# A one-token attention and MLP mix: the output row kept as four columns per partition and stored from there

## The chip, the cores and the metric

The kernel runs on one core of one Trainium2 chip. The metric is the device time of one execution in microseconds (us). The core has a matrix engine (TensorE, PE in the profile), VectorE (DVE), ScalarE (ACT), GpSimd (POOL) and SyncE (SP), each with its own stream of instructions; they meet only through semaphores. SP, ACT and POOL also issue DMAs, which sixteen DMA engines carry out. Matrix products take their weights and their moving data from the on-chip memory SBUF (128 partitions) and leave results in PSUM (128 partitions, eight banks).

## The reference, cut to what matters

One token `x` (512 numbers) goes through two branches, which a sigmoid gate `g` mixes. Branch A is attention with 32 heads of width 128 against a cache of 4096 keys and values per head; branch B is a two-layer MLP with a squared ReLU.

```python
g = sigmoid((x * gate_w).sum(-1, keepdims=True))
q = (x @ wq).reshape(32 heads, 128)
p = softmax(q @ k_cache^T * 128 ** -0.5)          # 32 x 4096
a = concat_heads(p @ v_cache) @ wo                # 4096 -> 512
h = relu(x @ w1 + b1) ** 2                        # 512 -> 1376
b = h @ w2 + b2                                   # 1376 -> 512
out = g * a + (1 - g) * b                         # 512 numbers, bf16
```

The two caches are 32 MiB each in bf16, `wq` and `wo` 4 MiB each, so the work is mostly the reading of some 78 MB.

## The kernel before, in words

The heads are taken in eight tiles of four (`NT = 8`). A ring of five slots of 4 MiB (`ring`, `SLOTS`) receives the K and V tiles in the order of `LOADS`; SP issues them, each when the slot's former owner has been used up (`free`). For a K tile DVE forms part of the scores itself (line 711) and PE turns the rest with a matmul against the identity (line 509) and multiplies it with the query columns (line 522); ACT forms the exponentials (line 434); PE multiplies with V (`pv`, line 553). The order on every engine is written out by hand in the blocks at the end of each engine's function.

The last stage is the one that the change touches. The output has 512 numbers, and the sums of all output products stand in one small PSUM tile, `acc`, 128 partitions by 4 columns: output number `n` is at partition `n % 128`, column `n // 128`. Five groups of products add to it, every one a 128 by 128 block of weights with one moving column, four blocks (`j = 0..3`) for the four columns:

- `out_a` (line 580): heads 0 to 27 with `wo`, for 22 of the 32 rows that a partition of `W` holds; the other ten rows are summed on DVE (`rows_v`, line 777) into `vsum` and added to `acc` by `add_v` (line 586), four fp32 matmuls with a column of ones.
- `mlp_out(n)` (line 605): the eleven blocks of `w2`; the first ten run before the last V products, the eleventh (`w2b`) at the very end.
- `out_b` (line 614): heads 28 to 31 with `wob_sb`, sixteen matmuls, after the last V products, their normalisation on DVE (`norm`, line 741) and the arrival of `wob_sb`.

The last three loads on SP's queue are the two parts of `wob_sb` (line 339) and `w2b` (line 341). PE's order at the end is: ten `mlp_out`, `pv(28)`, `add_v`, `pv(29)`, `pv(30)`, `pv(31)`, then `out_b`, then `mlp_out(10)`. Behind them the result is finished in four steps: DVE adds the gated bias `b2g` and rounds to bf16 (`fin`, line 814); PE turns the 128 by 4 tile into 4 rows of 128 (line 667); DVE copies these rows from PSUM to SBUF (`fin4`, line 816); SP stores the four rows, 256 bytes each (line 343), and waits for the store (line 819).

At the start, ACT issues four small loads, the last of which is `b2` as 4 rows of 128 (line 394); PE turns it into four columns with one small matmul (line 465), ahead of the eleven that turn `b1` (line 467) and of the query products (line 487).

Of the kernel before, what the change touches and what calls it, by code (L numbers as in the profile page):

```python
# [5 lines left out]
def bass_gated_mix__gqa_block_cached__dense_activation_squared_relu__decode_kernel(  # L6
# [15 lines left out]
    fp32 = mybir.dt.float32  # L22
# [7 lines left out]
    DM = 512  # L30
# [104 lines left out]
    with ctx:  # L135
# [21 lines left out]
        W4 = W3 + DM  # L157
        W5 = W4 + NZ * DM
        wob_sb = held("m")[:, W4:W5].rearrange("p (h n) -> p h n", h=NZ)
        oA, fin4 = [held("m")[0:p, W5 + n * 128:W5 + n * 128 + 128] for n, p in enumerate((NA, 4))]  # L160
        vsum = held("k", NT - 1)[:, 0:2 * DM].bitcast(fp32)


# [4 lines left out]
            at[0] += n  # L168
            return start[0:p, at[0] - n:at[0]]

        xrow, grow, b1r, b2r = early(1, DM), early(1, DM), early(1, F), early(4, 128)
        zeros = early(128, 128)
        xb = early(128, 4 * 128).rearrange("p (t n) -> p t n", t=4)

# [32 lines left out]
        b2g = sb("b2g", [128, 4], fp32)  # L207
        fin = sb("fin", [128, 4], bf16)

        KP = [pb(f"KP{i}", [128, HM * 128], bf16) for i in range(3)]  # L210
        pS = pb("pS", [128, 512], fp32)
        pM = pb("pM", [128, 512], fp32)
# [8 lines left out]
        Q = pM[:, 192:192 + NH]  # L221
        Z = pX[:, 0:1]
        XC = pO[:, 0:4]
        B2 = KP[2][:, 0:4]
        QR = [pQ, pX]
        H = pX[:, 256:256 + FG + 1]
        B1 = pM[:, 288:288 + FG + 1]
# [21 lines left out]
        s_at = sem("s_at")  # L249
        s_ac = sem("s_ac")  # L250
        s_b2 = sem("s_b2")
        s_fT = sem("s_fT")
        s_f4 = sem("s_f4")
        s_id = sem("s_id")
        s_cst = sem("s_cst")
        s_xc = sem("s_xc")
# [60 lines left out]
        @block.sync  # L317
        def _(eng):
            for n, (kind, j) in enumerate(LOADS):
                free(eng, n)  # L320
                if n == SLOTS - 1:
                    started(eng)
                    for p, st, k, q in STRIPS[len(RUNS):]:
                        a, b = W[p:p + st * (k - 1) + 1:st, :], woa_v[q:q + k, :]
                        if k == 1:
                            a, b = [v.rearrange("p (a n) -> p a n", a=2) for v in (a, b)]
                        eng.dma_start(a, b).then_inc(s_wr, 16)
                if kind == "v" and j in PARTS:
                    for w in range(len(PARTS[j]) - 1):
                        part = slice(PARTS[j][w] * 128, PARTS[j][w + 1] * 128)  # L330
                        eng.dma_start(held("v", j)[:, part], v_v[j][:, part]).then_inc(s_vl[j, w], 16)  # L331
                elif kind in "kv":
                    eng.dma_start(held(kind, j), (k_v if kind == "k" else v_v)[j])\
                       .then_inc(s_l[n % SLOTS], 16)
                elif kind == "m":
                    eng.dma_start(held("m")[:, 0:W2], w1_v).then_inc(s_w[0], 16)
                    eng.dma_start(held("m")[:, W2:W3], w2_v).then_inc(s_w[1], 16)  # L337
            for c in range(len(TS) - 1):
                eng.dma_start(wob_sb[:, TS[c]:TS[c + 1], :], wob_v[:, TS[c]:TS[c + 1], :])\
                   .then_inc(s_wo[c], 16)  # L340
            eng.dma_start(w2b, B_w2[F - 128:F, :]).then_inc(s_w[2], 16)
            eng.wait_ge(s_f4, 1)
            eng.dma_start(out[0, 0, :].rearrange("(j p) -> j p", p=128), fin4).then_inc(s_out, 16)


        @block.gpsimd
# [42 lines left out]
        @block.scalar  # L389
        def _(eng):  # L390
            eng.dma_start(xrow, A_x[0, :, :]).then_inc(s_x, 16)
            eng.dma_start(grow, gate_w.rearrange("(a n) -> a n", a=1)).then_inc(s_x, 16)
            eng.dma_start(b1r, B_b1.rearrange("(a n) -> a n", a=1)).then_inc(s_b, 16)
            eng.dma_start(b2r, B_b2.rearrange("(j p) -> j p", p=128)).then_inc(s_b, 16)
            eng.wait_ge(s_xc, 1)
            eng.activation(xcolf[:, :], XC, ACT.Copy).then_inc(s_xf, 1)
            eng.wait_ge(s_xf, 1)
            eng.activation(xcol[:, :], xcolf[:, :], ACT.Copy).then_inc(s_xf, 1)
            eng.wait_ge(s_z, 1)
            eng.activation(ez[:, :], Z, ACT.Exp, scale=-1.0).then_inc(s_ez, 1)  # L400

            def qb_copy(c):
                eng.wait_ge(s_qps, c + 1)
                for r in range(R):
                    rows = slice(P * r, P * r + P)
                    eng.activation(qb[rows, c, :], QR[c % 2][rows, r * 128:r * 128 + 128], ACT.Copy)\
                       .then_inc(s_qb, 1)

            def evac(u):
                for j in range(2):  # L410
                    n = 2 * u + j
                    if n >= NC:
                        eng.wait_ge(s_sh, n - NC + 1)
                    eng.wait_ge(s_t, n + 1)
                    eng.activation(kT[:, n % NC, 0:HB[u // U] * 128],  # L415
                                   KP[n % 3][:, 0:HB[u // U] * 128], ACT.Copy).then_inc(s_ev, 1)

            def sc_copy(j):
                eng.wait_ge(s_sh, 2 * U * (j + 1))
                for r in range(R):  # L420
                    rows = slice(P * r, P * r + P)
                    eng.activation(S[rows, j % NS, XT[j]:B], S2[j % 2][rows, r:U * YB[j] * R:R], ACT.Copy).then_inc(s_cp, 1)

            def exps(j):
                eng.wait_ge(s_mb, j + 1)
                eng.activation(nM[:, j:j + 1], MB[:, j:j + 1], ACT.Copy).then_inc(s_nm, 1)  # L426
                eng.wait_ge(s_nm, j + 1)
                if j == 0:
                    eng.wait_ge(s_cst, 3)
                if j >= NE:  # L430
                    eng.wait_ge(s_pv, U * (j - NE + 1))
                for r in range(R):
                    rows = slice(P * r, P * r + P)
                    eng.activation(E[rows, j % NE, :, r], S[rows, j % NS, :], ACT.Exp,  # L434
                                   bias=nM[rows, j:j + 1], scale=SCALE,
                                   accum_out=RS[rows, R * j + r:R * j + r + 1]).then_inc(s_e, 1)

            for c in range(EARLY):
                qb_copy(c)
            for i in range(NU + 2):  # L440
                if i >= U and i % U == 0:
                    sc_copy(i // U - 1)
                if i < NU:
                    evac(i)
                if i == NU - U:
                    exps(NT - 2)
                if EARLY + i < NT:
                    qb_copy(EARLY + i)
                if i > U and i % U == 1 and i != NU - U + 1:
                    exps(i // U - 1)  # L450
# [3 lines left out]
        def _(eng):  # L454
# [7 lines left out]
            eng.matmul(Z, onesf[0:1, :], zp[:, :], start=True, stop=True).then_inc(s_z, 1)  # L462
            eng.wait_ge(s_id, 4)
            eng.wait_ge(s_b, 32)
            eng.transpose(B2, b2r, ident[0:4, 0:4]).then_inc(s_b2, 1)
            for n in range(FG + 1):
                mm = eng.matmul(B1[:, n:n + 1], b1r[:, n:FG * 128:FG] if n < FG else b1r[:, F - 128:F],
                                ident[0:1, 0:1], start=True, stop=True)
# [114 lines left out]
            def add_v():  # L583
                eng.wait_ge(s_vs, TV)
                for j in range(4):
                    eng.matmul(acc[:, j:j + 1], vsum[:, j * 128:(j + 1) * 128], onesf[:, 0:1],
                               start=False, stop=False, skip_group_check=True)

            def mlp_h():
                eng.wait_ge(s_w[0], 16)  # L590
# [7 lines left out]
            def mlp_out(n):  # L598
                if n in (0, FG):
                    eng.wait_ge(s_w[1 if n < FG else 2], 16)  # L600
                if n == 0:
                    eng.wait_ge(s_hs, 1)
                w = w2a[:, n, :] if n < FG else w2b
                for j in range(4):
                    mm = eng.matmul(acc[:, j:j + 1], w[:, j * 128:(j + 1) * 128], hs[:, n:n + 1],
                                    start=False, stop=(n == FG), skip_group_check=True)
                if n == FG:
                    mm.then_inc(s_acc, 1)
# [1 line left out]
            def out_b(c):  # L610
                eng.wait_ge(s_wo[c], 16)
                for h in range(TS[c], TS[c + 1]):
                    for j in range(4):
                        eng.matmul(acc[:, j:j + 1], wob_sb[:, h, j * 128:(j + 1) * 128],  # L614
                                   onorm[:, NA + h:NA + h + 1], start=False, stop=False,
                                   skip_group_check=True)

# [40 lines left out]
            for u in range((NT - 1) * U, NU):  # L658
                if u == NU - 3:
                    add_v()  # L660
                pv(u)
            eng.wait_ge(s_on, NG)
            for c in range(len(TS) - 1):
                out_b(c)
            mlp_out(FG)
            eng.wait_ge(s_fin, 1)
            eng.transpose(KP[2][0:4, 0:128], fin[:, :], ident[:, :]).then_inc(s_fT, 1)


        @block.vector  # L670
        def _(eng):
# [20 lines left out]

            eng.wait_ge(s_b1, 1)
            eng.tensor_copy(b1c[:, :], B1).then_inc(s_b1c, 1)
            eng.wait_ge(s_dz, 3)
            eng.tensor_scalar(omw[:, :], omw[:, :], omg[:, 0:1], None, ALU.mult).then_inc(s_g, 1)

# [110 lines left out]
            gmax(NT - 1)  # L808
            rows_v()
            recip(NG - 1)  # L810
            norm(NG - 1)
            eng.wait_ge(s_acc, 1)
            eng.wait_ge(s_g, 4)
            eng.tensor_tensor(fin[:, :], acc[:, 0:4], b2g[:, :], ALU.add).then_inc(s_fin, 1)
            eng.wait_ge(s_fT, 1)
            eng.tensor_copy(fin4, KP[2][0:4, 0:128]).then_inc(s_f4, 1)

        inner.close()
        nc.sync.wait_ge(s_out, 16)
# [28 lines left out]
```

## Time and profile before

| what | us |
|---|---|
| median of 3 runs (193.01 to 193.13) | 193.02 |
| the profiled execution, its own time | 192.9 |
| span of the profiled execution | 191.5 |
| DVE busy in the span | 159.0 (83%) |
| PE busy in the span | 111.0 (58%) |
| data read from memory | 78.35 MB, 409 GB/s over the span |
| granted TensorE clock after the start | 0.5 of full speed |

The span is the stretch from the first to the last recorded instruction; the execution's own time lies 1.4 us above it. Section 2 of the page cuts the span into 40 slices of 4.8 us and gives each engine's busy share in tenths. The chain is the work that ended last, followed back from the end: every piece of it was released by the one before it. A line of the timeline gives the start, the duration, the engine, the source line, the operation, its tiles and, in brackets, how long the engine had been idle and what released it. PEld is the loading of weights into the matrix engine, SPq the queue on which SP issues DMAs.

### The profile page before, as it was taken

What the parts mean: (1) busy time and instruction counts of PE and PEld (TensorE: products, weight loads), DVE (VectorE), ACT (ScalarE), POOL (GpSimd) and SP (SyncE); (2) the same over time, 40 slices, a digit from 0 to 9 for tenths busy, and PEclk for the clock granted to TensorE, in tenths of its full rate; (3) what the DMA queues carried; (4) which work ended last, traced back from release to release, by engine and by line L of the source; (5) the groups of instructions that cost most, each with busy time, mean ns of one, the idle gap of its engine ahead of it and who ended that gap; (6) DMA issues with size and microseconds to landing.
All of it is one profiled execution on the core that took longest, in us unless ns stands there. A gap on an engine that the chain in (4) does not pass through costs nothing.

```text
span 191.5 us, 6005 instructions
## 1 busy us (share of the span) xinstructions
PE 111.0 (58%) x2058; PEld 97.6 (51%) x2058; DVE 159.0 (83%) x1387; ACT 82.7 (43%) x204; POOL 22.7 (12%) x56
## 2 busy tenths in 40 slices
PE   0129667545614653397569145933887478648975
PEld 0123335535503542297459145933877268537964
DVE  0320399999999999899999998998999799998821
ACT  2105765843833663087349222941663393000400
POOL 7760000996000000000000000000000000000000
PEclk9999985855555555555555555555555555555555
DMA  6999999999999999999999999999999999999992
GB/s 226 432 438 438 438 440 428 438 411 450 411 443 411 421 412 421 438 429 431 414 447 421 428 426 428 431 417 424 428 419 424 411 428 409 421 415 428 417 382 70
DMA packets 5488, 78.74 MB, mean 411 GB/s; under 512 B 1285, under 2 KB 1927, under 8 KB 2056
## 3 DMA queue, kind: packets, MB, share of 16 engines
q1 hardware_dynamic: 4484, 75.40, 92.9%
q0 software_dynamic: 960, 2.95, 3.9%
q8 instruction: 16, 0.26, 0.6%
q14 instruction: 14, 0.11, 0.1%
q10 hardware_dynamic: 14, 0.01, 0.0%
HBM read 78.35 MB, written 0.00 MB: 409 GB/s over the span
## 4 chain that ended last, share of the span: by engine, by line
DVE 48%; DMA 40%; SPq 7%; PE 3%; issue 1%; DVEq 0%
DVE ring L711 45%; DMA ring<-in_A_k_cache_dram 26%; DMA ring<-in_A_wo_dram 14%; SPq L331 6%; DVE S L711 2%; PE pO L553 1%; PE KP L509 1%; DVE gm L725 1%; DVE gx L728 0%; PE pM L562 0%; PE pM L534 0%; PE pQ L614 0%; SPq L337 0%; SPq L294 0%; DVE mp L718 0%
## 5 line engine op out<-in xcount | busy, mean ns | idle before, releaser
L711 DVE CUSTOM_DVE_ANT_0 ring<-ring,qb 128x128 bf16<-128x128 bf16 x656 | 140.6, 280 | 2.9 <-DMA ring<-in_A_k_cache_dram 2.9
L415 ACT ACTIVATE kT<-KP 128x768 bf16<-128x768 bf16 (+1 forms) x64 | 46.4, 783 | 48.1 <-PE KP L509 47.8
L509 PE MATMUL KP<-ident,ring 128*128 128x128 bf16 x368 | 43.4, 302 | 23.2 <-DMA ring<-in_A_k_cache_dram 19.9
L711 DVE DVE_READ_ACCUMULATOR2_ANT S<- 128x1 f32 x656 | 49.7, 76 | 0.1
L509 PEld LDWEIGHTS KP<-ident,ring 128*128 128x128 bf16 x368 | 36.0, 140 | 25.9 <-DMA ring<-in_A_k_cache_dram 20.4
L553 PE MATMUL pO<-E,ring 128*128 128x4 bf16 x640 | 19.5, 167 | 2.9 <-DMA ring<-in_A_v_cache_dram 1.9
L553 PEld LDWEIGHTS pO<-E,ring 128*128 128x128 bf16 x640 | 18.7, 105 | 3.4 <-DMA ring<-in_A_v_cache_dram 2.1
L434 ACT ACTIVATE E<-S,nM 32x128 bf16<-32x128 f32 x32 | 18.5, 580 | 0.9
L553 PE MATMUL pX<-E,ring 128*128 128x4 bf16 x384 | 12.0, 167 | 4.6 <-DMA ring<-in_A_v_cache_dram 4.6
L553 PEld LDWEIGHTS pX<-E,ring 128*128 128x128 bf16 x384 | 11.4, 105 | 5.1 <-DMA ring<-in_A_v_cache_dram 4.9
L426 ACT ACTIVATE nM<-pM 128x1 f32<-128x1 f32 x8 | 1.4, 172 | 23.0 <-PE pM L534 23.0
L529 PE MATMUL pM<-identf,mp 128*1 128x128 f32 x8 | 3.1, 384 | 13.0 <-DVE mp L718 13.0
L534 PE MATMUL pM<-onesf,gx 1*128 1x1 f32 x16 | 4.6, 357 | 8.9 <-DVE gx L728 8.9
L534 PEld LDWEIGHTS pM<-onesf,gx 1*128 1x128 f32 x16 | 4.0, 306 | 9.6 <-DVE gx L728 9.6
L522 PE MATMUL pQ<-qcol,kT 128*128 128x4 bf16 x176 | 7.8, 170 | 1.0 <-ACT kT L415 0.9
L522 PEld LDWEIGHTS pQ<-qcol,kT 128*128 128x128 bf16 x176 | 7.6, 111 | 1.4 <-ACT kT L415 1.4
L434 ACT ACTIVATION_READ_ACCUMULATOR E<-S,nM 32x1 f32 x32 | 8.1, 253 | 0.0
L522 PE MATMUL pS<-qcol,kT 128*128 128x4 bf16 x192 | 8.1, 169 | 0.0
L386 POOL MEMSET tick<- 1x1 f32 x1 | 0.1, 88 | 66.8 <-DMA W<-in_A_wo_dram 66.8
L378 POOL DMA_DIRECT2D W<-in_A_wo_dram x14 | 8.0, 572 | 0.0
L529 PEld LDWEIGHTS pM<-identf,mp 128*1 128x1 f32 x8 | 0.7, 92 | 14.2 <-DVE mp L718 14.0
L522 PEld LDWEIGHTS pS<-qcol,kT 128*128 128x128 bf16 x192 | 7.8, 108 | 0.2
(83 smaller groups left out, 97.3 us busy)
## 6 DMA issues: line engine op xcount, KB each, us to landing
ring<-in_A_k_cache_dram SPq DMA_DIRECT2D x8, 4096.0 KB, 30.4
ring<-in_A_v_cache_dram SPq DMA_DIRECT2D x5, 4096.0 KB, 29.7
W<-in_A_wq_dram SPq DMA_DIRECT2D x1, 4096.0 KB, 12.4
ring<-in_A_v_cache_dram SPq DMA_DIRECT2D x2, 2048.0 KB, 27.7
ring<-in_A_v_cache_dram SPq DMA_DIRECT2D x4, 1024.0 KB, 27.5
ring<-in_A_v_cache_dram SPq DMA_DIRECT2D x2, 1280.0 KB, 31.4
W<-in_A_wo_dram POOLq DMA_DIRECT2D x2, 768.0 KB, 17.8
ring<-in_B_w_dram SPq DMA_DIRECT2D x1, 1376.0 KB, 24.8
```

Of the source, the lines that this page charges most:

```text
L331: eng.dma_start(held("v", j)[:, part], v_v[j][:, part]).then_inc(s_vl[j, w], 16)
L378: eng.dma_start(W[p:p + st * (k - 1) + 1:st, :], woa_v[q:q + k, :], max_dma_last_dim=16384).then_inc(s_wp[n], 16)
L415: eng.activation(kT[:, n % NC, 0:HB[u // U] * 128], KP[n % 3][:, 0:HB[u // U] * 128], ACT.Copy).then_inc(s_ev, 1)
L426: eng.activation(nM[:, j:j + 1], MB[:, j:j + 1], ACT.Copy).then_inc(s_nm, 1)
L434: eng.activation(E[rows, j % NE, :, r], S[rows, j % NS, :], ACT.Exp, bias=nM[rows, j:j + 1], scale=SCALE, accum_out=RS[rows, R * j + r:R * ...
L509: mm = eng.transpose(KP[n % 3][:, y * 128:(y + 1) * 128], held("k", j)[:, b * 128:(b + 1) * 128], ident[:, :])
L522: mm = eng.matmul(S2[j % 2][:, c:c + R], kT[:, n % NC, y * 128:(y + 1) * 128], qcol[:, R * j:R * j + R], start=True, stop=True)
L529: eng.transpose(MT[0:1, :], mp[:, j:j + 1], identf[:, :]).then_inc(s_mt, 1)
L534: eng.matmul(MB[:, j:j + 1], gx[0:1, j % 2, :], onesf[0:1, 0:1], start=True, stop=True).then_inc(s_mb, 1)
L553: mm = eng.matmul(O(R * j, R * j + R), held("v", j)[:, b * 128:(b + 1) * 128], E[:, j % NE, b, :], start=(b == 0), stop=(b == B - 1), skip ...
L711: ins = eng.tensor_tensor_reduce(kb, kb, qb[:, j, :], 1.0, 0.0, ALU.mult, ALU.add, S[:, j % NS, b:b + 1])
L725: eng.tensor_reduce(g, MT[0:1, :].rearrange("a (r p) -> a r p", r=R), AX.X, ALU.max)\
```

## The change

The output is kept in another layout: output number `n` is at partition `n // 4`, column `n % 4`, so that partition `p` holds four neighbouring numbers, and the store takes them straight from `fin`, 128 partitions of 8 bytes.

- The products of the last stage, `out_b` and `mlp_out(10)`, take every fourth column of the weights (`j:DM:4`) and add to a new PSUM tile `last`, in this layout.
- All other products still go to `acc`, in the old layout. `add_v` now closes it and signals. DVE then forms `wide` (128 by 4 by 32, fp32): `acc` spread along a mask `four`, where `four[p, i]` is 1 for `p // 4 == i`. PE multiplies `wide` as weights with a second mask `rest` (`rest[p, j]` is 1 for `p % 4 == j`), which starts `last` with these sums in the new layout (`turn`). `wide` stands on DVE between the last `recip` and the last `norm`; `turn` on PE between `pv(29)` and `pv(30)`.
- The two masks are made on DVE at the start, by two reductions of the fp32 identity, behind the copy of `b1c`.
- `b2` is loaded as one row and turned into the new layout by four one-row matmuls, into `pS` in place of `KP[2]`.
- The turning matmul on PE, the copy to `fin4` on DVE and their two semaphores are gone.

```diff
-        oA, fin4 = [held("m")[0:p, W5 + n * 128:W5 + n * 128 + 128] for n, p in enumerate((NA, 4))]
+        oA = held("m")[0:NA, W5:W5 + 128]
+        wide = held("m")[:, W5 + 128:W5 + 384].bitcast(fp32).rearrange("p (j i) -> p j i", j=4)
...
-        xrow, grow, b1r, b2r = early(1, DM), early(1, DM), early(1, F), early(4, 128)
+        xrow, grow, b1r, b2r = early(1, DM), early(1, DM), early(1, F), early(1, DM)
...
+        four = sb("four", [128, 32], fp32)
+        rest = sb("rest", [128, 4], fp32)
...
-        B2 = KP[2][:, 0:4]
+        B2 = pS[:, 0:4]
+        last = pS[:, 64:68]
...
-            eng.wait_ge(s_f4, 1)
-            eng.dma_start(out[0, 0, :].rearrange("(j p) -> j p", p=128), fin4).then_inc(s_out, 16)
+            eng.wait_ge(s_fin, 1)
+            eng.dma_start(out[0, 0, :].rearrange("(p j) -> p j", p=128), fin[:, :]).then_inc(s_out, 16)
...
-            eng.dma_start(b2r, B_b2.rearrange("(j p) -> j p", p=128)).then_inc(s_b, 16)
+            eng.dma_start(b2r, B_b2.rearrange("(a n) -> a n", a=1)).then_inc(s_b, 16)
...
-            eng.transpose(B2, b2r, ident[0:4, 0:4]).then_inc(s_b2, 1)
+            for t in range(4):
+                mm = eng.matmul(B2[:, t:t + 1], b2r[:, t:DM:4], ident[0:1, 0:1], start=True, stop=True)
+            mm.then_inc(s_b2, 1)
...
             def add_v():
                 eng.wait_ge(s_vs, TV)
                 for j in range(4):
-                    eng.matmul(acc[:, j:j + 1], vsum[:, j * 128:(j + 1) * 128], onesf[:, 0:1],
-                               start=False, stop=False, skip_group_check=True)
+                    mm = eng.matmul(acc[:, j:j + 1], vsum[:, j * 128:(j + 1) * 128], onesf[:, 0:1],
+                                    start=False, stop=True, skip_group_check=True)
+                mm.then_inc(s_cv, 1)
+
+            def turn():
+                eng.wait_ge(s_wd, 1)
+                eng.matmul(last, wide[:, :, :].rearrange("p j i -> p (j i)"), rest[:, :],
+                           start=True, stop=False, skip_group_check=True)
...
-                w = w2a[:, n, :] if n < FG else w2b
                 for j in range(4):
-                    mm = eng.matmul(acc[:, j:j + 1], w[:, j * 128:(j + 1) * 128], hs[:, n:n + 1],
+                    w = w2a[:, n, j * 128:(j + 1) * 128] if n < FG else w2b[:, j:DM:4]
+                    mm = eng.matmul((acc if n < FG else last)[:, j:j + 1], w, hs[:, n:n + 1],
                                     start=False, stop=(n == FG), skip_group_check=True)
...
-                        eng.matmul(acc[:, j:j + 1], wob_sb[:, h, j * 128:(j + 1) * 128],
+                        eng.matmul(last[:, j:j + 1], wob_sb[:, h, j:DM:4],
...
+                if u == NU - 2:
+                    turn()
                 pv(u)
...
-            eng.wait_ge(s_fin, 1)
-            eng.transpose(KP[2][0:4, 0:128], fin[:, :], ident[:, :]).then_inc(s_fT, 1)
...
+            eng.wait_ge(s_id, 4)
+            eng.tensor_reduce(four[:, :], identf[:, :].rearrange("p (i j) -> p i j", j=4), AX.X, ALU.max)\
+               .then_inc(s_fr, 1)
+            eng.tensor_reduce(rest[:, :], identf[:, :].rearrange("p (i j) -> p j i", j=4), AX.X, ALU.max)\
+               .then_inc(s_fr, 1)
...
             recip(NG - 1)
+            eng.wait_ge(s_cv, 1)
+            eng.wait_ge(s_fr, 2)
+            eng.tensor_tensor(wide[:, :, :], acc[:, 0:4].unsqueeze(2).to_broadcast([128, 4, 32]),
+                              four[:, :].unsqueeze(1).to_broadcast([128, 4, 32]), ALU.mult).then_inc(s_wd, 1)
             norm(NG - 1)
             eng.wait_ge(s_acc, 1)
             eng.wait_ge(s_g, 4)
-            eng.tensor_tensor(fin[:, :], acc[:, 0:4], b2g[:, :], ALU.add).then_inc(s_fin, 1)
-            eng.wait_ge(s_fT, 1)
-            eng.tensor_copy(fin4, KP[2][0:4, 0:128]).then_inc(s_f4, 1)
+            eng.tensor_tensor(fin[:, :], last, b2g[:, :], ALU.add).then_inc(s_fin, 1)
```

## The prediction

> **What bounds the kernel now.** I read the page's slices first, then the chain in order of time near its end, then the timeline of the last microseconds, and last the DMA view of the store.
>
> The slices say that the whole span but its last slice is DMA-bound: the DMA row stands at 9 nearly everywhere, and the granted TensorE clock (PEclk) is 0.9 and more in the first five slices (to 24 us) and 0.5 from the ninth on.
>
> ```profile
> PEclk9999985855555555555555555555555555555555
> DMA  6999999999999999999999999999999999999992
> ```
>
> The chain says what is left when the loads run out. Columns are start, duration, what. A load of the last weights lands at 188.56; from there to the store it is 16 products, 4 products, the add, the turning matmul and the copy.
>
> ```profile
> 162.59 25.97 DMA ring<-in_A_wo_dram
> 188.56 0.14 issue
> 188.70 0.57 PE pQ L614 x16
> 189.26 0.28 PE pQ L605 x4
> 189.54 0.02 issue
> 189.57 0.17 DVE fin L814
> 189.74 0.04 issue
> 189.78 0.28 PE KP L667
> 190.07 0.02 issue
> 190.09 0.21 DVE ring L816
> ```
>
> The timeline has the store's issue, the list of waits has SP's last one (0.4 us, for the store), and the DMA view from 190.3 to 191.5, in 40 slices of 0.03 us, the store's eight packets (four of data, four that signal): they run from 191.08 to 191.17, and the span ends at 191.5.
>
> ```profile
> 190.33 0.29 SPq L343 DMA_DIRECT2D out_dram<-ring  x1
> ...
> SPq L819 <- DMA out_dram<-ring: 0.4, 1, 0.4
> ...
> GB/s 0 0 0 0 0 0 0 0 0 0 0 0 0 0 0 0 0 0 0 0 0 0 0 0 0 0 17 9 9 0 0 0 0 0 0 0 0 0 0 0
> ...
> q1 hardware_dynamic: 8, 0.00, 0.5%
> ```
>
> So the store takes 191.5 - 190.33 = 1.17 us from issue to end, and everything that the change does to the end is in 188.56 to 191.5. One wait is not in the chain: `w2b` is issued at 172.27 and its row for line 341 says 16.9 us to landing, which is 189.2. The four `mlp_out` products start at 189.26 because of that load, not because of the sixteen before them.
>
> **Part 1, removed: the turning matmul and the copy.** The store now waits for `fin` (end 189.74) in place of the copy (190.09 + 0.21 = 190.30). Nothing lies beside these steps. The gap from release to issue, 0.03, stays. Term: 189.74 - 190.30 = **-0.56 us**, and SP issues at 189.77.
>
> **Part 2, the strided weights.** The trace has weights with a step of ten elements (lines 594 and 467) and of four (line 459), and contiguous ones (line 614):
>
> ```profile
> 8.11 0.26 PE L459 MATMUL pO<-ident,ring 1*128 1x1 bf16 x4 [8.11 <-DMA ring<-in_gate_w_dram]
> 13.12 0.74 PE L467 MATMUL pM<-ident,ring 1*128 1x1 bf16 x11
> 176.83 2.60 PE L594 MATMUL pX<-xcol,ring 128*128 128x1 bf16 x44
> 188.70 0.57 PE L614 MATMUL pQ<-onorm,ring 128*128 128x1 bf16 x16 [0.55 <-DMA ring<-in_A_wo_dram]
> ```
>
> The pace is (stretch - one duration) / (count - 1), with durations 0.167, 0.192, 0.197 and 0.165 of the source views: step four 31 ns, step ten 55 and 56 ns, contiguous 27 ns. Step ten has one pace at a granted clock of 1.0 (13 us, one row of weights) and of 0.5 (177 us, 128 rows), so neither clock nor rows enter, and the row with the same step, 31 ns, is the nearest. The sixteen products then need 188.67 + 16 x 0.031 = 189.17, still before `w2b` at 189.2: nothing. The four behind it: 4 x 0.004 = **+0.02**. The upper end is 56 ns: the sixteen end at 188.67 + 16 x 0.056 = 189.57, 0.31 after 189.26, and the four cost 4 x 0.029 = 0.12, together +0.43. The lower end is 0.
>
> The Trainium skill, SBUF — State Buffer, section "Door 1: The DMA port swizzle", says that accesses run at full bandwidth with at least two hits in a 16-byte line. A step of four bf16 is 8 bytes, two hits; a step of ten is 20 bytes, one. By that rule the term is 0 and the sum moves by 0.02; the rows at 31 and 56 ns fit it, but no row here has 128 partitions with step four.
>
> **Part 3, the store of 128 pieces of 8 bytes.** This is the unknown. Its shape, 128 partitions spread over all sixteen engines with eight packets each, is in the trace only as a load, `wq` at the start: issue 0.74, duration 0.40. Counted in the DMA view in windows that begin at 0.7, its queue has 7 packets by 1.85, 11 by 2.0, 14 by 2.15, 15 by 2.3 and the sixteenth engine's first by 2.7. Three things grow:
> - The issue: 0.40 against 0.29, +0.11 (the shortest 128-partition issue of the timeline, line 336, is 0.33: +0.04).
> - The engines: four of them start, work and signal within 0.09 us here, about 0.02 each; sixteen at that step, 0.32, are +0.24. Lower end 0 (all at once). Upper end by `wq`: its last engine starts up to 2.7 - 0.74 = 1.96 after the issue, the store's last packet 191.17 - 190.33 = 0.84: +1.1 with the issue counted.
> - The packets: 0.5% of 16 engines in 1.2 us is 0.096 us for eight, 12 ns each; nine on an engine in place of two: +0.08.
>
> Ends: +0.04 + 0.08 = +0.1, and +1.1 + 0.08 = about +1.2. A gain is excluded, since issue, engines and packets all go up in number. `wq` is the first load of a cold core and reads 32 KB pieces, so I stay nearer the store's own row: 0.11 + 0.24 + 0.08 = **+0.42** after rounding.
>
> **Part 4, `wide` and `turn`: cost nothing.** `add_v` ends at 184.99. `wide` is 128 x 128 fp32 elements; the nearest row, line 718, reduces as many in 0.285, so it ends near 185.3. DVE's only later work is the last `norm`, which starts at 188.26 after 5.10 us of idleness. On PE `turn` follows `pv(29)`:
>
> ```profile
> 184.85 1.21 PE L553 MATMUL pO<-E,ring 128*128 128x4 bf16 x40
> ...
> 186.71 0.24 PE L553 MATMUL pO<-E,ring 128*128 128x4 bf16 x3 [0.66 <-DMA ring<-in_A_v_cache_dram]
> ```
>
> PE is free from 186.06 to 186.71, waiting for V. `turn` is one fp32 product, two passes as line 562 (0.59 for two, 128x4): 186.06 + 0.59 = 186.65. Cover 0.06, at worst; behind it the V products end near 188.15 and `norm` at 188.48, 0.08 before the load at 188.56. If both covers went, every 0.1 us that `turn` is late would cost at most 0.1.
>
> **Part 5, the start: cost nothing.** Three more one-row matmuls (3 x 0.03 = 0.1) stand ahead of `b1` and the query products; two reductions of 0.285 on DVE, which idles 3.21 us before 17.46. The end of this stage is DVE's wait for the first K tile, idle 1.36 us before 22.70, and that absorbs both. The row `b2` takes one packet on one engine where it took four packets on four; it shares a semaphore with `b1` and is again last on ACT's queue. If it came later, the first 1.36 us would be covered too.
>
> **Sum.** -0.56 + 0.02 + 0.42 = -0.12 on the profiled execution's 192.9. The median, 193.02, is 0.12 above that execution; I apply the sum to the median: **192.9 us**. The barrier between SP and the other engines is no new end: PE and DVE finish earlier than before too.
>
> **The rivals.**
> - *The store stays as cheap as it is* (chance 0.20). For it: the packets are short and the wait after them (191.17 to 191.5) is the longest part, which has no reason to multiply. Against it: sixteen engines must all signal. Store +0.1: -0.56 + 0.02 + 0.1 = -0.44, **192.6**. The Trainium skill, DMA: Bandwidth & Descriptors, section "Anatomy of one DMA", takes this side: the fixed cost is mostly the confirmation of the last write, and many descriptors can be emitted before their number shows. It says so for the GpSimd path, and no run here shows it for SP's.
> - *The store of 8-byte pieces is slow* (0.18). Place: between SP's issue and its last wait. For it: the spread of `wq` over its engines; against it: cold start. With +1.2 the sum is -0.56 + 0.02 + 1.2 = +0.66, **193.7**; it makes the kernel slower by over 0.2% from a store of +0.93 on. The same page, section "Specifications", says that pieces under 512 B are read, modified and written; the old store's 256 B are under it as well, so the count of them, 128 for 4, is what it would add.
> - *Strided weights at the pace of step ten* (0.10). For it: 128 partitions, as line 594; against it: line 459. -0.56 + 0.43 + 0.42 = +0.29, **193.3**, which is still within 0.2%.
>
> **How the numbers follow.** My forecast has the remaining 0.52. 0.2% is 0.39 us, about what a measurement of this kernel can tell from no change. Forecast and strided weights lie within it (0.62), the cheap store is faster by more (0.20), the slow store slower by more (0.18). The forecast alone would be 192.7 to 193.2. The range takes in the cheap store's end and the slow store's: 192.5 to 193.7.
>
> **What would show it.** In the profile after: the store's issue follows `fin` by 0.03; `last` products at 31 ns each, the four of `mlp_out(10)` still released by the load of `w2b`; `turn` ending before 186.7; packets of the store, 128 + 16, spread over 0.3 to 0.4 us, and issue to end near 1.6 us. The prediction is wrong if that last figure is under 1.3 or over 2.1, if the products' pace is near 56 ns, or if the landing of the last loads moves from 188.56 and 189.2, which nothing in the change asks for.

## The result and the profile after

The changed kernel takes 194.07 us (median of 6 runs, 193.88 to 194.41) against 193.01 (192.93 to 193.14): slower by 0.57%, ratio 1.0057 with a 95% interval of 1.0047 to 1.0067. The profiled execution took 194.09, its span is 192.8 (before: 192.9 and 191.5).

The chain of the changed kernel, in order of time (start, duration, what), still begins its end with the last `wo` load, which lands at 188.68 here (188.56 before):

```profile
162.70 25.98 DMA ring<-in_A_wo_dram
188.68 0.14 issue
188.81 0.67 PE pS L628 x16
189.48 0.16 PE pS L619 x4
189.64 0.02 issue
189.66 0.16 DVE fin L837
```

After `fin` there is nothing but the store. The timeline shows its issue, SP's waits show the last one, and the DMA view from 189.8 to 192.8, in 40 slices of 0.075 us, shows its packets (16 x 8 of data and 16 that signal) and the time from issue to landing in the last column:

```profile
189.85 0.35 SPq L349 DMA_DIRECT2D out_dram<-fin  x1
...
SPq L840 <- DMA out_dram<-fin: 2.2, 1, 2.2
...
GB/s 0 0 0 0 0 0 0 0 0 0 0 0 8 6 1 0 0 0 0 0 0 0 0 0 0 0 0 0 0 0 0 0 0 0 0 0 0 0 0 0
...
q1 hardware_dynamic: 144, 0.00, 2.6%
...
out_dram<-fin SPq DMA_DIRECT2D x1, 1.0 KB, 2.9
```

Little of the 2.9 us is moving data. All 144 packets run between 190.70 and 190.92, in three slices. Then nothing moves until the span ends, at 192.78 to two places of the trace: 1.86 us in which SP only waits for the signals, by which the engines confirm that their writes are done. Before, the same wait after the last packet was 191.17 to 191.53, 0.36 us (the prediction has 0.33, from the rounded end). The trace also records when each of the sixteen signals arrives. The first six come from 191.10 to 191.23, as promptly after the packets as those of the old store (191.43 to 191.49); the other ten come later, spread out from 191.70 to 192.74. So the confirmation is not one long delay for all engines: ten of them are late, each by another amount.

The two parts that were to be hidden are hidden. `wide` and `turn` in the timeline of the changed kernel:

```profile
185.08 0.29 DVE L832 TENSOR_TENSOR ring<-pQ,four 128x128 f32<-128x128 f32 x1 [1.87 <-PE pQ L594]
185.95 0.50 PEld L600 LDWEIGHTS pS<-rest,ring 128*128 128x128 f32 x2
185.97 0.57 PE L600 MATMUL pS<-rest,ring 128*128 128x4 f32 x2
186.76 1.37 PEld L561 LDWEIGHTS pO<-E,ring 128*128 128x128 bf16 x48 [0.31 <-DMA ring<-in_A_v_cache_dram]
```

`turn` ends at 186.54 and PE then still waits 0.2 us for V.

The account of the two profiled spans: SP issues the store at 189.85 in place of 190.33 (-0.48, of which the two steps gone are -0.56 or so and the later load gives back about 0.1), and the store takes 192.78 - 189.85 = 2.93 in place of 191.53 - 190.33 = 1.20 (+1.73). Together that is +1.25, as much as the spans differ (192.78 - 191.53).

### The profile page after: what moved, and what is told of

It reads as the page before. It is cut to its first block, busy times and chain, and to the rows that moved or that the text cites. A ratio compares the mean times of both kernels' runs of the same rounds, so it can differ in the third digit from the quotient of the medians.

```text
span 192.8 us, 6016 instructions
## 1 busy us (share of the span) xinstructions
PE 109.5 (57%) x2062; PEld 97.0 (50%) x2062; DVE 159.4 (83%) x1389; ACT 82.8 (43%) x204; POOL 22.6 (12%) x56
## 4 chain that ended last, share of the span: by engine, by line
DVE 48%; DMA 39%; SPq 7%; PE 3%; issue 1%; DVEq 0%
DVE ring L730 44%; DMA ring<-in_A_k_cache_dram 26%; DMA ring<-in_A_wo_dram 13%; SPq L337 6%; DVE S L730 2%; PE pO L561 1%; SPq L343 1%; PE KP L517 1%; DVE gm L744 1%; DVE gx L747 0%; PE pS L628 0%; PE pM L542 0%; PE pM L570 0%; DVE mp L737 0%; SPq L300 0%
## 5 line engine op out<-in xcount | busy, mean ns | idle before, releaser
L517 PE MATMUL KP<-ident,ring 128*128 128x128 bf16 x368 | 42.9, 299 | 22.2 <-DMA ring<-in_A_k_cache_dram 18.9
L730 DVE DVE_READ_ACCUMULATOR2_ANT S<- 128x1 f32 x656 | 50.4, 77 | 0.0
L517 PEld LDWEIGHTS KP<-ident,ring 128*128 128x128 bf16 x368 | 35.4, 138 | 24.6 <-DMA ring<-in_A_k_cache_dram 19.4
```

The costliest lines, as they stand in the source:

```text
L517: mm = eng.transpose(KP[n % 3][:, y * 128:(y + 1) * 128], held("k", j)[:, b * 128:(b + 1) * 128], ident[:, :])
L730: ins = eng.tensor_tensor_reduce(kb, kb, qb[:, j, :], 1.0, 0.0, ALU.mult, ALU.add, S[:, j % NS, b:b + 1])
```

## Which part loses the time: the store, or the rest

Theory R: the store waits for the confirmation of 128 small writes, and everything else of the change is covered. Theory K: sixteen engines that must signal are what costs. Theory E: half or more comes from the earlier parts.

**The store alone, in the kernel before.**

```diff
-            eng.wait_ge(s_f4, 1)
-            eng.dma_start(out[0, 0, :].rearrange("(j p) -> j p", p=128), fin4).then_inc(s_out, 16)
+            eng.wait_ge(s_fin, 1)
+            eng.dma_start(out[0, 0, :].rearrange("(p j) -> p j", p=128), fin[:, :]).then_inc(s_out, 16)
...
-            eng.transpose(KP[2][0:4, 0:128], fin[:, :], ident[:, :]).then_inc(s_fT, 1)
...
-            eng.tensor_copy(fin4, KP[2][0:4, 0:128]).then_inc(s_f4, 1)
```

> The kernel before with nothing changed but its end: the turning matmul and the copy are left out, and fin is stored from its columns as 128 pieces of 8 bytes (the 512 numbers land in another order, so the output's order is what this kernel changes). Theory R (the store waits for 128 small writes to memory to be confirmed; everything else of the change is hidden): the two steps gone are -0.57, the store grows from 1.17 to about 2.9 us, +1.74, so 194.1 to 194.3 us, as slow as the changed kernel or a little slower. Theory K (it is the number of engines that have to signal, 16 in place of 4): the same, 194.1 to 194.3. Theory E (half or more of the loss comes from earlier parts, the strided weights, wide, turn, the start): 193.6 us or less.

Measured: 193.94 us against 192.80 for the kernel before beside it, ratio 1.0057 (1.0042 to 1.0072), the same loss as the whole change. That is 0.16 us under the range that R and K named, as the kernel before took 0.2 us less beside these runs than beside the first (193.01). Its store again takes 192.6 - 189.70 = 2.9 us:

```profile
189.70 0.35 SPq L343 DMA_DIRECT2D out_dram<-fin  x1
...
SPq L815 <- DMA out_dram<-fin: 2.2, 1, 2.2
```

Theory E falls.

**Everything but the store.**

```diff
-            eng.wait_ge(s_fin, 1)
-            eng.dma_start(out[0, 0, :].rearrange("(p j) -> p j", p=128), fin[:, :]).then_inc(s_out, 16)
+            eng.wait_ge(s_f4, 1)
+            eng.dma_start(out[0, 0, :].rearrange("(j p) -> j p", p=128), fin4).then_inc(s_out, 16)
...
             mlp_out(FG)
+            eng.wait_ge(s_fin, 1)
+            eng.transpose(KP[2][0:4, 0:128], fin[:, :], ident[:, :]).then_inc(s_fT, 1)
...
             eng.tensor_tensor(fin[:, :], last, b2g[:, :], ALU.add).then_inc(s_fin, 1)
+            eng.wait_ge(s_fT, 1)
+            eng.tensor_copy(fin4, KP[2][0:4, 0:128]).then_inc(s_f4, 1)
```

> The changed kernel with everything of the change but its store: fin is turned by a matmul, copied and stored as 4 rows of 256 bytes as before (in this layout the numbers land in another order, which is what this kernel changes of the output). Theories R and K: the loss is gone, 193.0 to 193.2 us (the strided products' 0.02 to 0.1 stay). Theory E: 193.5 us or more.

Measured: 193.06 against 192.80, ratio 1.0016 (1.0006 to 1.0025). So the store is the loss, with at most 0.25% left for the rest. Four later runs looked for that rest.

> The kernel before with only the weights of the last twenty products strided (every fourth column, in out_b and the last mlp_out; they add to the old layout, so the sums are mixed up, which is what it changes of the output). Theory S0 (the strided pace, 33 ns, is hidden behind the last load but for 0.02 us): within 0.1 us of the kernel before. Theory S1 (the 0.2 to 0.3 us that the changed kernel loses with its old end come from the strided products): 0.2 to 0.3 us slower than before.

```diff
-                w = w2a[:, n, :] if n < FG else w2b
                 for j in range(4):
+                    w = w2a[:, n, j * 128:(j + 1) * 128] if n < FG else w2b[:, j:DM:4]
...
-                        eng.matmul(acc[:, j:j + 1], wob_sb[:, h, j * 128:(j + 1) * 128],
+                        eng.matmul(acc[:, j:j + 1], wob_sb[:, h, j:DM:4],
```

> The kernel before with only the start of the change: b2 as one row and four small matmuls, and the two masks on DVE, which nothing uses (the bias is added in the wrong order, which is what it changes of the output). Theory C (covered by the wait for the first K tile): within 0.1 us of the kernel before, and the 0.2 to 0.3 us that the changed kernel loses with its old end lie at wide and turn, or in the moved place of the code loads. Theory B (the start shifts the stream of loads): 0.2 us or more slower.

```diff
-            eng.transpose(B2, b2r, ident[0:4, 0:4]).then_inc(s_b2, 1)
+            for t in range(4):
+                mm = eng.matmul(B2[:, t:t + 1], b2r[:, t:DM:4], ident[0:1, 0:1], start=True, stop=True)
+            mm.then_inc(s_b2, 1)
...
+            eng.tensor_reduce(four[:, :], identf[:, :].rearrange("p (i j) -> p i j", j=4), AX.X, ALU.max)\
+               .then_inc(s_fr, 1)
...
```

> The changed kernel with the old end and with contiguous weights in its last twenty products: what is left of the change is its start, wide and turn (the last products stand in another order than the turned sums, which is what it changes of the output). Theory T (wide and turn cost the 0.2 to 0.3 us that the changed kernel with the old end was slower): 0.2 to 0.3 us slower than before. Theory C (no part costs anything by itself; it was the combination or the chips' scatter): within 0.1 us.

Against the kernel with the old end above:

```diff
-                    w = w2a[:, n, j * 128:(j + 1) * 128] if n < FG else w2b[:, j:DM:4]
+                    w = (w2a[:, n, :] if n < FG else w2b)[:, j * 128:(j + 1) * 128]
...
-                        eng.matmul(last[:, j:j + 1], wob_sb[:, h, j:DM:4],
+                        eng.matmul(last[:, j:j + 1], wob_sb[:, h, j * 128:(j + 1) * 128],
```

> The changed kernel with the old end once more, for a narrower interval. Theory T: 0.2 to 0.3 us slower than before, as measured first (0.06 to 0.25%). Theory C: under 0.15 us.

| kernel | us | before beside it | ratio (95%) |
|---|---|---|---|
| only strided weights | 192.78 | 192.86 | 0.9997 (0.9988 to 1.0005) |
| only the start | 192.86 | 192.94 | 0.9999 (0.9990 to 1.0008) |
| start, `wide` and `turn` | 193.01 | 192.86 | 1.0008 (0.9999 to 1.0017) |
| all but the store, again | 192.92 | 192.86 | 1.0004 (0.9995 to 1.0013) |

None of the parts, and not their sum the second time, stands clear of zero. The two readings of all parts but the store are +0.16% and +0.04%, about 0.1% or 0.2 us together, against the 0.57% of the whole change; whether that 0.1% is real these runs can't tell. Theories S1 and B fall, since 0.2 us lies outside their intervals. Theory T is not quite excluded: the kernel with the start, `wide` and `turn` is 0.15 us slower, between T and C, with an interval that holds both, and the second reading of all parts, 0.06 us, speaks for C. The pace of the strided products is read directly in the changed kernel: sixteen in 0.67 us, (0.67 - 0.172) / 15 = 33 ns each.

## Engines, or pieces

**Sixteen engines with one piece of 64 bytes each.**

```diff
+        fin4 = held("m")[0:16, W5 + 128:W5 + 160]
...
-            eng.dma_start(out[0, 0, :].rearrange("(j p) -> j p", p=128), fin4).then_inc(s_out, 16)
+            eng.dma_start(out[0, 0, :].rearrange("(j p) -> j p", p=32), fin4).then_inc(s_out, 16)
...
-            eng.tensor_copy(fin4, KP[2][0:4, 0:128]).then_inc(s_f4, 1)
+            eng.tensor_copy(fin4, KP[2][0:16, 0:32]).then_inc(s_f4, 1)
```

> The kernel before, but its last copy takes 16 partitions by 32 columns of the turned tile, and the store writes 16 pieces of 64 bytes on sixteen engines (12 of the 16 rows hold leftovers: the output's values are what is left out). Theory R: few writes, so the store stays near 1.2 to 1.4 us and the kernel at 193.0 to 193.2 us. Theory K: sixteen engines signal, the store takes about 2.8 us and the kernel 194.4 to 194.7 us.

**Four engines with 32 pieces of 8 bytes each.**

```diff
-            eng.dma_start(out[0, 0, :].rearrange("(j p) -> j p", p=128), fin4).then_inc(s_out, 16)
+            eng.dma_start(out[0, 0, :].rearrange("(a j b) -> j a b", j=4, b=4), fin4.rearrange("j (a b) -> j a b", b=4)).then_inc(s_out, 16)
```

> The kernel before, but each of the four rows is written as 32 pieces of 8 bytes, so 4 engines write 128 pieces (the numbers land in another order). Theory R: the confirmations take as long as in the changed kernel, store about 2.7 to 3.2 us (with some 0.3 us for 33 packets on an engine), kernel 194.5 to 195.0 us. Theory K: 4 signals as before, store 1.4 to 1.5 us, kernel 193.2 to 193.4 us.

Measured: sixteen engines 192.97 us, ratio 1.0008 (0.9998 to 1.0017); four engines 194.98, ratio 1.0110 (1.0095 to 1.0125). The issue and SP's last wait, first of the sixteen engines' kernel, then of the four engines':

```profile
190.30 0.35 SPq L344 DMA_DIRECT2D out_dram<-ring  x1
...
SPq L820 <- DMA out_dram<-ring: 0.6, 1, 0.6
```

```profile
190.61 0.30 SPq L343 DMA_DIRECT2D out_dram<-ring  x1
...
SPq L819 <- DMA out_dram<-ring: 2.3, 1, 2.3
```

From issue to the span's end that is 191.7 - 190.30 = 1.4 and 193.7 - 190.61 = 3.1 us. Theory K falls on both sides: sixteen engines are cheap with one piece each, four are dear with 32.

## What it is about the pieces

> The kernel before, and behind its last wait 24 more stores from SBUF into a scratch tensor, each waited for before the next is issued: twelve shapes, twice over. (Its own time is of no interest; the time of each store from issue to the end of its wait is.) Known so far: 128 x 8 B about 2.9 us, 16 x 64 B about 1.35, 4 x 256 B about 1.2. Theory R1 (neighbouring small writes into the same stretch of memory wait for each other): 128 x 8 B with a step of 512 B takes 1.4 us or less, with a step of 64 B somewhere between; 64 x 16 B about 2, 32 x 32 B about 1.6; 128 x 16 B and 128 x 32 B shorter than 128 x 8 B, 128 x 64 B about 1.4. Theory R2 (each small piece costs some 13 ns by itself, wherever it goes): the steps change nothing, 2.9 us each; 128 x 64 B down to 1.4 us. Theory R3 (the number of pieces alone counts): every store of 128 pieces, 8 to 512 B, takes 2.7 us or more, 64 pieces 2.0, 32 pieces 1.6. All: 16 x 8 B about 1.4 us.

The edit, one of 24 such pairs of lines behind the kernel's last wait (`src` is a tile of exponentials, `pr` a scratch tensor):

```diff
+        nc.sync.dma_start(pr[0:512].rearrange('(p j) -> p j', p=128), src[:, 0:4]).then_inc(s_p[0], 16)
+        nc.sync.wait_ge(s_p[0], 16)
```

Three of the answers by source line, each with the issue's duration in ns and the time from issue to landing. Line 823 stores 128 packed pieces of 8 bytes, line 825 the same pieces with a step of 64 bytes, line 829 packed pieces of 16 bytes:

```profile
L823 SPq DMA_DIRECT2D probe_dram<-E x1: 345/345/345, 191.4 to 191.4; - x1
DMA to landing us min/median/max: 3.3/3.3/3.3
...
L825 SPq DMA_DIRECT2D probe_dram<-E x1: 320/320/320, 194.7 to 194.7; - x1
DMA to landing us min/median/max: 1.4/1.4/1.4
...
L829 SPq DMA_DIRECT2D probe_dram<-E x1: 320/320/320, 197.5 to 197.5; - x1
DMA to landing us min/median/max: 1.4/1.4/1.4
```

The same number of pieces, engines and signals, from the same source, takes 3.3 us or 1.4. So it is not the number of pieces (theory R3), and not each small piece by itself (theory R2): 8-byte pieces are quick when they lie apart. R1 stands as far as small pieces near each other go, but its middle figures were wrong, since 16 bytes were enough.

> The kernel before, and behind its last wait twenty more stores into a scratch tensor, each waited for before the next: ten shapes, twice over. Known from the first probe, from issue to landing: 128 x 8 B packed 3.3 us, the same pieces with a step of 64 or 512 B 1.4, 128 packed pieces of 16, 32, 64 B 1.4, 16 x 8 B packed 1.3. Theory G (two pieces that share a stretch of 16 bytes wait for each other): step 16 B and step 32 B 1.4; 64 x 8 B packed about 2.3 and 32 x 8 B about 1.8; 128 x 4 B packed 3 us or more; 128 x 12 B, 128 x 24 B and 128 x 16 B off by 8 bytes all clearly over 1.4, up to 3; the order of the pieces over the engines changes nothing (3.3). Theory L (more than four pieces in a stretch of 64 bytes wait for each other): step 16 B 1.4; 24 B and off by 8 bytes 1.4 to 1.6; 12 B between; 64 x 8 B 2.3. Theory S (only pieces next to each other on one engine wait): with each engine's pieces 128 B apart the packed store falls to about 1.5; the store of 4 engines (3.1 us) speaks against it.

> The kernel before, and behind its last wait eight more shapes of stores into a scratch tensor, twice over. Known, from issue to landing: packed pieces of 8 B 3.2 to 3.7 us (128 of them), 3.8 to 4.6 (64), 4.4 to 4.8 (32), 1.3 (16, one on each engine); 128 x 12 B 3.3, 128 x 24 B 2.0 to 2.6, 16 B and its multiples 1.4, 16 B off by 8 bytes 1.5, 8 B with a step of 16 B 1.6 to 1.8. Theory M (a piece whose length is no multiple of 16 bytes is read, mixed and written, and waits for an earlier one nearby): 20 B and 14 B pieces 2 us or more; 64 x 8 B with a step of 16 B 1.4 to 1.8; even and odd pieces at once from SP and ACT 3 us or more; 32 x 8 B with a step of 64 B 1.4; 32 x 16 B 1.4. Theory D (it is the density of pieces alone, however long): 20 B 1.4, 32 x 16 B 1.8 or more.

Both probes have the form of the first, with other slices; even and odd pieces at once are `src[0:127:2, 0:4]` from SP and `src[1:128:2, 0:4]` from ACT. All shapes, issue to landing in us, both times that each was done in its kernel (4 x 256 B from its issue to the next):

| store | us | store | us |
|---|---|---|---|
| 128 x 8 B, packed | 3.3, 3.4; 3.2, 3.7; 3.1, 3.3 | 128 x 16 B | 1.4, 1.4 |
| 64 x 8 B, packed | 3.8, 4.6 | 128 x 16 B, off by 8 bytes | 1.5, 1.5 |
| 32 x 8 B, packed | 4.8, 4.4; 3.3, 3.1 | 128 x 32 B and 128 x 64 B | 1.4, 1.4 |
| 16 x 8 B, packed | 1.3, 1.3 | 128 x 512 B | 1.5, 1.5 |
| 128 x 8 B, step 16 B | 1.8, 1.6 | 64 x 16 B (issue 0.5) | 1.7, 1.7 |
| 128 x 8 B, step 32 B | 1.4, 1.7 | 32 x 16 B | 2.0, 2.0 |
| 128 x 8 B, step 64 and 512 B | 1.4, 1.4 | 32 x 32 B and 16 x 64 B | 1.3, 1.3 |
| 128 x 8 B, packed, neighbours eight partitions apart | 3.9, 3.6 | 128 x 20 B | 2.0, 2.4 |
| 128 x 4 B, packed | 8.9, 8.6 | 128 x 24 B | 2.0, 2.6 |
| 128 x 12 B, packed | 3.4, 3.3 | 128 x 14 B | 2.3, 2.2 |
| 64 even and 64 odd pieces of 8 B at once | 3.1, 3.2 | 64 even pieces of 8 B alone | 2.0, 1.6 |
| 32 x 8 B, step 64 B | 1.4, 1.4 | 4 x 256 B | 1.15, 1.14 |

What follows: 32 to 128 packed pieces of 4 to 12 bytes are slow (3 us and more), packed pieces of 16, 32 and 64 bytes quick where there are 128 of them. Theory G falls, for pieces of 16 bytes that are off by 8 share every stretch of 16 bytes and are quick. Theory S falls by the pieces whose neighbours stand eight partitions apart (that such neighbours are on different engines is inferred: the trace does not show which engine writes which piece). Theory L falls by 24 bytes (slow, three or four in 64 bytes) and by the shifted 16 (quick, five). Theory M has 20, 14 and 24 bytes for it and 32 x 16 B at 2.0 against it; theory D has it the other way round. Odd too is that 32 and 64 packed pieces of 8 bytes (3.1 to 4.8 us) take no less than 128; theories G and L had put them at 1.8 and 2.3. So length and closeness both enter. The signals show the same picture as in the changed kernel: of a slow store some arrive on time and the others one after another, for the second packed store of 32 x 8 B in the last probe nine by 1.25 us after the issue, then 1.68, 2.09, 2.10, 2.12, 2.53, 3.11 and 3.12. That looks like writes that wait for each other in turn, but by what mechanism **stays open**. Not tested is whether engines that write into the same stretch of memory are what waits: shared evenly, 32 x 16 B gives each of sixteen engines 32 bytes, the quick 32 x 32 B and 64 x 16 B 64 bytes; but the four engines above had 256 bytes each and were slow.

> The changed kernel with its store alone changed: fin has eight columns, four of them zero, and is stored as 128 packed pieces of 16 bytes into a scratch tensor of 2 KB (the output itself gets the input row, written early on, so the result is left out of it). Same engines, same number of pieces and signals, same place in the kernel. Theory P (packed pieces under 16 bytes are what is slow): store from issue to end 1.4 to 1.5 us in place of 2.9, kernel 1.4 us faster than the changed one, 192.5 to 192.8 us, at or below the kernel before. Theory N (128 pieces on sixteen engines are slow at the end of this kernel whatever their size, and the quick ones of the probe were quick because nothing ran beside them): 193.8 us or more.

```diff
+        fin = sb("fin", [128, 8], bf16)
...
+            eng.dma_start(pr[0:1024].rearrange("(p j) -> p j", p=128), fin[:, :]).then_inc(s_fo, 16)
...
+            eng.tensor_tensor(fin[:, 0:4], last, b2g[:, :], ALU.add).then_inc(s_fin, 1)
```

Measured: 192.65 against 192.86, ratio 0.9988 (0.9980 to 0.9997). The store's issue, and in the DMA view from 189.8 to 191.4 the same 144 packets, now 1.4 us from issue to landing:

```profile
189.91 0.33 SPq L353 DMA_DIRECT2D probe_dram<-fin  x1
...
q1 hardware_dynamic: 144, 0.00, 4.8%
...
probe_dram<-fin SPq DMA_DIRECT2D x1, 2.0 KB, 1.4
```

Theory N falls and P holds. Here the sixteen signals all arrive from 191.14 to 191.31. With the length of the pieces doubled (and a scratch tensor as the target, into which pieces of 8 bytes took 3.1 to 3.7 us above), the changed kernel is faster than the one before, by some 0.2 us: what the change took off the end was real, and the store's confirmation ate it and 1.1 us more. (This kernel's 2 KB are not the output, so it is no version to use.)

## Two attempts at a version that keeps the gain

**Two queues.**

> The changed kernel whose store is issued in two halves at once, the even partitions' pieces from SP and the odd ones' from ACT, each 64 pieces of 8 bytes with a step of 16 bytes. Theory M1 (only neighbours in one store, on one queue, wait for each other): each half takes about 1.7 us, kernel 192.8 to 193.1 us, no slower than before. Theory M2 (neighbours wait wherever they come from): store 2.8 us or more, kernel 193.9 us or more.

```diff
+            halves = out[0, 0, :].rearrange("(p c j) -> c p j", c=2, j=4)
+            eng.dma_start(halves[0], fin[0:127:2, :]).then_inc(s_out, 16)
...
+            eng.wait_ge(s_fin, 1)
+            eng.dma_start(halves[1], fin[1:128:2, :]).then_inc(s_out, 16)
```

Measured: 194.48 us, ratio 1.0079 (1.0065 to 1.0093), slower than the changed kernel. Its DMA view has the two halves, 2.3 and 3.5 us from issue to landing:

```profile
out_dram<-fin SPq DMA_DIRECT2D x1, 0.5 KB, 2.3
out_dram<-fin ACTq DMA_DIRECT2D x1, 0.5 KB, 3.5
```

M1 falls, and M2 has the time right: two queues do not help, so the waiting is not confined to one queue. That the halves wait because they are neighbours is not shown, as two stores at once whose pieces lie apart were not run.

**A turn on DVE, pieces of 64 bytes.**

> A version of my own, with the old layout: fin is written into columns 0, 8, 16 and 24 of a tile of 128 by 32, DVE turns it in blocks of 32 by 32, and every eighth partition of the result, 16 rows of 64 bytes, is stored (4 by 4 by 32 numbers on the side of the output). Gone are the matmul and the copy, 0.57 us; new are one DVE turn of 128 by 32, 0.15 to 0.25 us with its wait, and a store of 16 pieces, 0.17 us longer than the old one by store_16x64. Theory R (the number and size of pieces set the store): 0.1 to 0.25 us faster than the kernel before, 0.05 to 0.13%. Theory K (engines): with sixteen engines slower by over 1 us; it fell already. If the 64-byte pieces cost more when four engines write them: no gain or a loss of up to 0.2 us.

```diff
+            eng.dma_start(out[0, 0, :].rearrange("(j b i) -> b j i", b=4, j=4),
+                          finT[0:121:8, :]).then_inc(s_out, 16)
...
+            eng.tensor_tensor(fin[:, 0:32:8], acc[:, 0:4], b2g[:, :], ALU.add).then_inc(s_fin, 1)
+            eng.wait_ge(s_fin, 1)
+            eng.transpose(finT[:, :], fin[:, :]).then_inc(s_f4, 1)
```

Measured: 193.14 against 192.86, ratio 1.0013 (1.0003 to 1.0022). The timeline shows why:

```profile
189.51 0.17 DVE L816 TENSOR_TENSOR fin<-pQ,b2g 128x4 bf16<-128x4 f32 x1 [1.06 <-PE pQ L607]
189.72 0.21 DVE L818 STREAM_TRANSPOSE finT<-fin 128x32 bf16<-128x32 bf16 x1
189.96 0.64 SPq L344 DMA_DIRECT2D out_dram<-finT  x1
```

The turn costs the 0.21 expected and the store is issued at 189.96, 0.37 earlier than before (0.06 of it because the last `wo` load landed earlier, at 188.50). But a store of 4 by 4 by 32 takes SP 0.64 us to issue, where the plain ones took 0.29 to 0.35, and ends 1.7 after its issue (span 191.7) in place of 1.2. Theory R named the pieces and forgot the issue. No version here beats the kernel before.

## Why the prediction was wrong, by its steps

The forecast was 192.9 us, between 192.5 and 193.7; the kernel takes 194.07.

- *What bounds the kernel*: right. The stream of loads ends at the same place within 0.12 us, and only the tail behind it moved.
- *Part 1, -0.56*: right. `fin` ends at 189.82, the store is issued 0.03 later; the turning matmul and the copy are gone.
- *Part 2, +0.02 for the strided weights*: right in size, 33 ns against the 31 taken from the row of line 459. Its sign that `w2b` still releases the last four did not come: before, they began 0.16 us after the last of the sixteen (189.10, 189.26), now 0.03 (189.31, 189.34), which is the products' own pace. `w2b` lands at about 172.38 + 16.9 = 189.3, so the sixteen now end about when it lands and not before it. That cost nothing: all twenty are done 0.96 us after the last `wo` load, before 0.98. Alone, these weights cost nothing that can be told (0.9997). The Trainium skill's rule (SBUF — State Buffer, "Door 1: The DMA port swizzle"), no loss with two hits in a 16-byte line, has the order right but not the whole size at 128 partitions: 33 ns for a step of 8 bytes against 27 contiguous and 56 for a step of 20 bytes.
- *Part 3, +0.42 for the store, between +0.1 and +1.2*: **this step failed**; the store grew by 1.73, outside its own ends, and its 2.9 us lie beyond the 2.1 that the prediction gave as a sign of being wrong. The three things that were priced, at 0.43 together, grew by 0.23: the first packet starts 0.85 us after the issue in place of 0.75 (0.06 of this is the issue, priced at 0.11), and the packets run over 0.22 us in place of 0.09. The other 1.50 is the wait behind the last packet, from 0.36 to 1.86 us, which the sum put at nothing. The first rival says of it that it "has no reason to multiply", and the upper end, too, was made of issue, spread and packets alone. The runs show that wait to hang on how long the written pieces are and how close they lie; why is open.
- *Parts 4 and 5, nothing*: right as far as can be told, by `turn`'s end at 186.54, before V, and by the runs with those parts alone (0.9999 and 1.0008).
- *The rivals*: the slow store had the place and the sign, but its support, `wq`'s spread over the engines, was the wrong one, as the sixteen engines with 64 bytes show; its price, 1.2 for 1.73, was short by 0.5. Of the Trainium skill's two sentences (DMA: Bandwidth & Descriptors), "Anatomy of one DMA" makes the confirmation of the last write the largest part of a cost that is about constant, for the GpSimd path. On SP's queue here the wait after the last packet is 0.36 of the old store's 1.20 us, not the largest part, and 1.86 of the new one's 2.93, so not constant. That it changes with the pieces is why the rival drawn from the page was wrong. "Specifications", with its limit of 512 bytes, points the right way, but 128 pieces of 16 to 64 bytes, all below that limit, land in 1.4 us: the number of pieces below it is not the measure.

## What to carry to other kernels

Price a store at the end of a kernel in three parts, the issue, the packets and the confirmation after the last packet, and read the last as a wait of its own: a DMA view that goes silent long before the wait ends is the sign. 128 packed pieces of 8 or 12 bytes to memory took about 2 us more here than 128 of 16, 32 or 64 bytes (pieces of 20 and 24 bytes lay between), so 0.56 us spent on turning a tile into a few long rows was well spent. And a row of the trace with the same shape is no bound if it runs in the other direction: `wq` told what 128 pieces cost to read, and nothing of what they cost to write.

## What was not expected of the hardware

- The last confirmation of 128 packed 8-byte writes comes 1.86 us after the last packet, six of the sixteen within 0.35; 128 packed 4-byte writes make a store of 8.6 to 8.9 us; and 32 packed 8-byte pieces (3.1 to 4.8 us) are no quicker than 128 (3.1 to 3.7).
- The issue on SP depends on the shape of the pieces: 0.25 to 0.29 us for four rows, 0.32 to 0.35 for 128, about 0.5 for 64 and 0.64 for 4 by 4 by 32.
- A step of ten elements in the weights costs twice the contiguous pace, 56 against 27 ns, at a granted clock of 1.0 and of 0.5; a step of four 33, measured at 0.5.
